# Attention loads in a fused attention, mixture and feed-forward kernel: v in four buffers a step sooner, converted blocks in two buffers

## The chip, the cores and the metric

The kernel runs on one core of a Trainium2 chip, as one launch. The metric is the device time of one execution in microseconds. The profile is of one execution, whose span runs from its first to its last instruction.

## What is computed

Three layers follow one another. The attention is a linear one with decay: for each of 4 batches and 8 heads, over 768 positions of width 64, in blocks of 64,

```python
intra = einsum('bhic,bhjc->bhij', qb, kb) * Dmask
out   = einsum('bhij,bhjd->bhid', intra, vb) + einsum('bhid,bhde->bhie', qb * lam_pow, kv_state)
kv_state = lam_block * kv_state + einsum('bhsd,bhse->bhde', kb * rev_pow, vb)
```

Its output, read as 3072 tokens of width 512, goes through a soft mixture of 8 experts (4 slots each, inner width 1024: logits against `phi`, a softmax over tokens that forms the slots, `relu(slot @ w1) @ w2` for each expert, a softmax over slots that spreads the results), and then through a feed-forward layer of width 2048 with the gate `h * sigmoid(1.702 h)`. The weights `w_in` and `w_out` of this last layer arrive as float64 bit patterns and are turned into float32 on the chip.

## The kernel before

**Attention.** A step takes one batch, one half of a sequence (`HS` = 384 rows, in three chunks of 128) and one pair of heads; there are `NSTEP` = 32 steps. Four steps with the same half form a group `g`; even groups are first halves, odd groups second halves. The order of all instructions is written out by hand in the loop at L534, which is a software pipeline: at step `i` it issues, among others, the scores of step i+1 (`do_SC`, TensorE L300, masked by VectorE at L303), the transposes of q and k of step i+2 (`do_T`, L262 and L264, copied out by ScalarE at L272 and L275), the transposes of step i-1's result (`do_XT`, L358), the product with the state (`do_XS`, L339), the state update of step i+1 (`do_ST`, TensorE L313 with v and the decayed k, then VectorE L322 and L324), the decayed k of step i+2 (`do_kd`, ScalarE L288) and the product with v of step i (`do_XA`, L347). In the first step of a group the logits and the slot sums of an earlier group come on top (`tail_logits` L368, `tail_z` L455, `tail_slot` L440, `tail_acc` L449); in the other steps there is less of such tail work. Each engine runs its instructions in the order in which they are issued.

**Loads.** Nearly all loads go through SP's queue, in order; a load into a buffer that is still in use waits there and holds those behind it. At step i SP issues q of step i+5 (L123), a piece of the expert weights (512 KB, L159 or L161, into one of 32 slots of 4 KB a partition), k of step i+5 (two loads, L128; three buffers, freed by `do_kd` of step i), in odd steps a float64 block (`load_early`, L228), and v of step i+3 (two loads, L128; three buffers, freed by `do_XA` of step i). v of step i+3 is first read by `do_ST` in step i+2.

**The float64 blocks.** Ten blocks (`EARLY`, 128 x 256 values; eight of `w_in`, two of `w_out`) are converted beside the attention. They all pass through one tile, `stage`, which is the first of the 32 weight slots and holds the block and a third part for the result's bits. Block c is loaded at step 2c+1 and converted at step 2c+2 (`do_early`): ScalarE takes the magnitude (L183), VectorE puts the bits together in three instructions (L192, L195, L198), GpSimd makes a mask of the magnitude (L205) and multiplies by it (L206). The weight piece 31, the last in the first round of slots, reuses the slot of `stage`.

**After attention.** At the last steps the pools of attention are freed and more slots are laid over them. The experts (L757, L775) read the pieces of weights; 64 pieces are loaded in all, the rest of them as buffers come free. Then follow the output stages (L1013 and L1179), bound to TensorE.

Of the kernel before, what the change touches and what calls it, by code (L numbers as in the profile page):

```python
# [8 lines left out]
F32 = mybir.dt.float32  # L9
F32R = mybir.dt.float32r  # L10
U32 = mybir.dt.uint32
# [6 lines left out]
def attention_moe_gelu_kernel(  # L18
# [14 lines left out]
    PE, ACT, DVE, POOL, SP = nc.tensor, nc.scalar, nc.vector, nc.gpsimd, nc.sync  # L33

    B, H, S, D = q.shape
    P = 128
# [13 lines left out]
    NSTEP = NG * NHP  # L50
    NE = 1
    NPC = 32
# [14 lines left out]
    CB = 256  # L67
# [5 lines left out]
    slots = slots_cm.__enter__()  # L73
# [3 lines left out]
    attn = attn_cm.__enter__()  # L77

    early_cm = tc.tile_pool(name="early", bufs=2, side="right", reuse_waits="tile")
    early = early_cm.__enter__()  # L80
# [27 lines left out]
    q_r, q_t, k_t, v_t = {}, {}, {}, {}  # L108

    def step_of(s):  # L110
        g, hp = divmod(s, NHP)
        b, hf = divmod(g, NHF)
        return b, hf, hp, g

    def load_step(s, what="qkv"):
        if s >= NSTEP:
            return
        b, hf, hp, g = step_of(s)
        t0 = hf * HS
        if "q" in what:  # L120

            q_r[s] = early.tile([P, 2, R * D], F32, tag="qr", name="qr", bufs=3)
            SP.dma_start(out=q_r[s], in_=q[b, 2 * hp:2 * hp + 2, t0:t0 + HS, :].rearrange("h (p c) d -> p h (c d)", p=P))  # L123
        for src, nm, ts, bufs, pool in ((k, "k", k_t, 3, early), (v, "v", v_t, 3, attn)):
            if nm in what:
                t = pool.tile([P, R, 2, D], F32, tag=nm, name=nm, bufs=bufs)
                for h in range(2):
                    SP.dma_start(out=t[:, :, h, :],  # L128
                                 in_=src[b, 2 * hp + h, t0:t0 + HS, :].rearrange("(c p) d -> p c d", p=P))
                ts[s] = t  # L130

    w_in32, w_out32 = w_in.bitcast(U32), w_out.bitcast(U32)
    staged = {}


    PC = 1024
# [42 lines left out]
    def convert_abs(key, mask=None):  # L179
        if mask is None:  # L180
            mask = ex.tile([P, DM], F32, tag="cvm", name="cvm", bufs=3)
        m = mask
        ACT.activation(out=m, in_=staged[key][:, :, 1].bitcast(F32), func=AF.Abs)  # L183
        magn[key] = m

    def conversion(key, out, guard):


        t, m = staged.pop(key), magn.pop(key)
        up, low = t[:, :, 1], t[:, :, 0]  # L190
        a = out.bitcast(U32) if key[0] != "early" else stage[:, 2 * CB:3 * CB]
        DVE.tensor_scalar(out=a, in0=up, scalar1=3, scalar2=0x3FFFFFFF,  # L192
                          op0=ALU.logical_shift_left, op1=ALU.bitwise_and)
        yield
        DVE.scalar_tensor_tensor(out=a, in0=up, scalar=0xC0000000, in1=a,  # L195
                                 op0=ALU.bitwise_and, op1=ALU.bitwise_or)
        yield
        DVE.scalar_tensor_tensor(out=a, in0=low, scalar=29, in1=a,  # L198
                                 op0=ALU.logical_shift_right, op1=ALU.bitwise_or)
        yield  # L200
        if guard is DVE:
            DVE.scalar_tensor_tensor(out=out, in0=m, scalar=F64_MIN, in1=a.bitcast(F32),
                                     op0=ALU.is_ge, op1=ALU.mult)
        else:
            POOL.tensor_scalar(out=m, in0=m, scalar1=F64_MIN, scalar2=None, op0=ALU.is_ge)  # L205
            POOL.tensor_tensor(out=out, in0=a.bitcast(F32), in1=m, op=ALU.mult)  # L206

    def by_turns(*work, rounds=9):

        work = list(work)  # L210
        while work and rounds:
            work = [w for w in work if next(w, 0) is None]
            rounds -= 1
        return work


    stage = slots.tile([P, PC], F32, tag="w", name="stage").bitcast(U32)

    NCW = 512 // CB

    EARLY = [(w_in32, kk * P, n * 512 + h * CB, w_in_sb[n][:, kk, h * CB:(h + 1) * CB])
             for n in range(NE) for kk in range(KD) for h in range(NCW)]
# [2 lines left out]

    def load_early(c):
        src, r, o, dst = EARLY[c]
        SP.dma_start(out=stage[:, :2 * CB], in_=src[r:r + P, 2 * o:2 * (o + CB)])  # L228
        staged["early", c] = stage[:, :2 * CB].rearrange("p (n t) -> p n t", t=2)

    def do_early(c):
        o = EARLY[c][-1]
        convert_abs(("early", c), o)
        by_turns(conversion(("early", c), o, POOL))
# [247 lines left out]
    with tc.manual_schedule():  # L482
# [7 lines left out]
        def warm_up(n):  # L490
            for _ in range(n):
                PE.matmul(bwarm, warm[:, :P], warm, start=True, stop=True)
# [5 lines left out]
        for h in range(2):  # L498
            r = slice(h * D, (h + 1) * D)
# [10 lines left out]
        n = 1  # L510
# [12 lines left out]
        def make_isum():  # L523
            for j in range(G):
                for i in range(G):
                    POOL.tensor_copy(out=isum4[i * NS:(i + 1) * NS, j, :],
                                     in_=ident[i * NS:(i + 1) * NS, i * NS:(i + 1) * NS])

        def load_pieces(i):
            n = min(NPC, max(0, i + 1) * NPC // (NSTEP - 1), NPC - 1 if i < NSTEP - 5 else NPC)  # L530
            while nxt_w[0] < n:
                load_piece()

        for i in range(-2, NSTEP):  # L534
            g, ph = divmod(i, NHP)
            if i > -2:
                load_step(i + 5, "q")
            if i == 1:
                make_isum()

            if 0 <= i + 1 < NSTEP:
                do_SC(i + 1)
            if 0 < i + 2 < NHP:

                for h in range(2):
                    make_dec(2 * (i + 2) + h)

            if 0 <= i + 2 < NSTEP:
                do_T(i + 2)
                if i == -2:  # L550
                    warm_up(1)
            if i == NSTEP - 1:
                do_XS(i)
            if 0 <= i - 1 < NSTEP:
                do_XT(i - 1)
            if 0 <= i + 3 < NSTEP:
                do_q(i + 3)
            if ph == 1 and 0 <= g - 1 < NG:
                tail_L(g - 1)
            if ph == 2 and 0 <= g - 1 < NG:  # L560
                tail_max(g - 1)
            if ph == 3 and 0 <= g - 1 < NG:
                tail_exp(g - 1)
            if i == NSTEP - 1:
                tail_logits_first(NG - 1)
            if 0 <= i < NSTEP - 1:
                do_XS(i)

            if 0 <= i + 1 < NSTEP:
                do_ST(i + 1)  # L570
            if 0 <= i + 2 < NSTEP:
                do_kd(i + 2)
            if 0 <= i < NSTEP:
                do_XA(i)

            if ph == 0 and 0 <= g - 1 < NG:
                tail_logits(g - 1)
            if ph == 0 and 0 <= g - 2 < NG:
                tail_z(g - 2, "tk")
                tail_slot(g - 2)  # L580
                tail_acc(g - 2)
            if i == NSTEP - 4:
                load_pieces(i + 1)

            load_pieces(i)

            load_step(i + 5, "k")
            c, turn = divmod(i - 2, EVERY)
            if turn == 1 and 0 <= c + 1 < len(EARLY):
                load_early(c + 1)  # L590
            if i >= 0:
                load_step(i + 3, "v")
            if 0 <= i + 2 < NSTEP:
                do_qd(i + 2)
            if i == -2:
                load_step(2, "v")
                SP.dma_start(out=phi_sb, in_=phi.rearrange("(k p) s -> p k s", p=P))
            if turn == 0 and 0 <= c < len(EARLY):
                do_early(c)
            if ph == 3 and 0 <= g - 1 < NG and i < NSTEP - 1:  # L600
                tail_row(g - 1)
            if ph == 0 and 0 <= g - 2 < NG:
                tail_row_exp(g - 2)
            if i == NSTEP - 2:
                early_cm.__exit__(None, None, None)
                slotb_cm = tc.tile_pool(name="slotb", bufs=NPC_B, side="right", reuse_waits="tile")
                slotb = slotb_cm.__enter__()

                rooms = [piece_room(NPC + j) for j in reversed(range(NPC_B))]
                while rooms:  # L610
                    load_piece(rooms.pop())
            if i == NSTEP - 1:
                attn_cm.__exit__(None, None, None)
                slotc_cm = tc.tile_pool(name="slotc", bufs=NPC_C, side="left", reuse_waits="tile")
                slotc = slotc_cm.__enter__()
                for _ in range(NPC_C):
                    load_piece()
# [288 lines left out]
        for kk in range(KD):  # L906
            src = bso[kk][:, None, :NS].to_broadcast([P, G, NS])
# [447 lines left out]
```

## Time and profile before

| | us |
|---|---|
| runs | 482.38, 485.71, 1572.84 (median 485.71) |
| the profiled execution | 483.99 |
| its span | 482.2 |
| TensorE busy in the span | 470.6 (98%) |
| VectorE busy | 375.5 (78%) |
| ScalarE busy | 302.8 (63%) |
| GpSimd busy | 76.4 (16%) |

The run of 1572.84 us is far from the others and is not used. The profiled execution lies between the two others. Busy shares are means over the whole span, in which attention, experts and output stages follow one another; matmuls are pipelined, so that a busy TensorE can still be waiting in between. The granted clock of TensorE is full over the span (mean 0.998). In the rows below, L12 is line 12 of the kernel; PEld is TensorE's weight load, SPq the sequencer of SP; a matmul group is named by the tile it writes (`bs` scores, `bst` state update, `bx` output, `bq` and `bk` transposes, `bp` slot sums).

### The profile page before, as it was taken

How to read it: one execution, taken by the hardware profiler on the slowest of the kernel's cores; microseconds unless marked ns; L12 is line 12 of the kernel's file. 1: busy time of each engine (PE TensorE's matmuls, PEld its weight loads, DVE VectorE, ACT ScalarE, POOL GpSimd, SP SyncE). 2: the span in 40 equal slices, each digit the busy share in tenths (PEclk: the TensorE clock that was granted, in tenths of full speed). 3: DMA queues.
4: the chain of work that ended last, by engine and by line, in shares of the span. 5: the costliest groups of instructions: out<-in, count | busy, mean ns of one | idle time of the engine just before them, and what ended most of it. 6: DMA issues, size and time to landing. Idle time of an engine off the chain costs nothing.

```text
span 482.2 us, 10665 instructions
## 1 busy us (share of the span) xinstructions
PE 470.6 (98%) x3991; PEld 391.7 (81%) x3991; DVE 375.5 (78%) x903; ACT 302.8 (63%) x605; POOL 76.4 (16%) x125
## 2 busy tenths in 40 slices
PE   8998999999999999999999999999999999999996
PEld 5877778778887443878788778888899999999996
DVE  4777778988875432897787598998779988888986
ACT  5786677777774126876865867676756565565551
POOL 3553344443230110000000000000001111011101
PEclk9999999999999999999999999999999999999999
DMA  8999989999899999246644542100222331233024
GB/s 185 250 286 275 270 256 293 282 260 295 235 306 354 410 407 369 89 159 238 220 130 130 189 133 98 63 0 2 88 88 36 54 44 15 32 45 45 4 43 88
DMA packets 81796, 81.52 MB, mean 169 GB/s; under 512 B 54736, under 2 KB 63440, under 8 KB 81744
## 3 DMA queue, kind: packets, MB, share of 16 engines
q1 hardware_dynamic: 79296, 76.63, 50.8%
q0 software_dynamic: 2304, 4.20, 6.4%
q8 instruction: 32, 0.52, 0.5%
q14 instruction: 20, 0.16, 0.1%
q10 hardware_dynamic: 144, 0.00, 0.0%
HBM read 69.80 MB, written 11.01 MB: 168 GB/s over the span
## 4 chain that ended last, share of the span: by engine, by line
PE 76%; DMA 12%; DVE 7%; SPq 2%; issue 1%; ACT 1%; DVEq 0%; ACTq 0%
PE bo L1013 26%; PE bp L1179 24%; DMA w<-in_moe_w_dram 9%; PE bs L300 4%; PE bx L347 3%; PE bx L339 2%; PE bsh L1135 2%; PE bhh L966 2%; PE bst L313 2%; DMA v<-in_v_dram 2%; PE bq L262 2%; PE bt L358 1%; SPq L128 1%; DMA stage<-in_moe_w_in_dram 1%; PE bk L264 1%
## 5 line engine op out<-in xcount | busy, mean ns | idle before, releaser
L1013 PE MATMUL bo<-wlo,GHI 128*128 128x512 f32 x192 | 75.3, 395 | 0.1
L1013 PE MATMUL bo<-whi,GLO 128*128 128x512 f32 x192 | 75.1, 394 | 0.0
L1013 PE MATMUL bo<-whi,GHI 128*128 128x512 f32 x192 | 74.8, 393 | 0.1
L1149 ACT ACTIVATE GHI<-G_all 128x896 fp32r<-128x896 f32 x48 | 45.8, 954 | 46.1 <-DVE G_all L1142 45.9
L1142 DVE TENSOR_TENSOR G_all<-G_all 128x128 f32<-128x128 f32 x192 | 47.4, 288 | 18.5 <-ACT G_all L1138 15.9
L1209 POOL DMA_DIRECT2D out_dram<-f x16 | 14.2, 1046 | 279.7 <-DVE G_all L1142 265.1
L1179 PE MATMUL bp<-tc,GHI 128*128 128x256 f32 x288 | 55.9, 282 | 0.0
L1154 DVE TENSOR_TENSOR GLO<-G_all,GHI 128x896 fp32r<-128x896 f32 x48 | 52.0, 1084 | 0.0
L974 ACT ACTIVATE G_all<-bhh 128x384 f32<-128x384 f32 x64 | 28.2, 489 | 34.6 <-PE bhh L966 34.5
L1179 PE MATMUL bp<-whi,GHI 128*128 128x256 f32 x192 | 49.5, 281 | 0.0
L1179 PE MATMUL bp<-wlo,GHI 128*128 128x256 f32 x192 | 49.2, 282 | 0.0
L1179 PE MATMUL bp<-whi,GLO 128*128 128x256 f32 x168 | 47.5, 283 | 0.0
L1179 PEld LDWEIGHTS bp<-tc,GHI 128*128 128x128 f32 x288 | 44.4, 190 | 0.0
L1013 PEld LDWEIGHTS bo<-wlo,GHI 128*128 128x128 f32 x192 | 36.0, 188 | 9.6 <-issue 2.5
L1013 PEld LDWEIGHTS bo<-whi,GLO 128*128 128x128 f32 x192 | 36.0, 188 | 7.8 <-DVE GLO L980 0.3
L1013 PEld LDWEIGHTS bo<-whi,GHI 128*128 128x128 f32 x192 | 36.1, 188 | 7.5 <-DVE W2s L920 0.5
L1179 PE MATMUL bp<-tc,GLO 128*128 128x256 f32 x144 | 40.4, 280 | 0.0
L980 DVE TENSOR_TENSOR GLO<-G_all,GHI 128x768 fp32r<-128x768 f32 x32 | 30.6, 955 | 10.5 <-ACT GHI L977 10.2
L281 POOL TENSOR_TENSOR qdT<-qT,qtab 128x384 f32<-128x384 f32 x32 | 32.1, 1002 | 38.7 <-PE bx L339 17.8
L300 PEld LDWEIGHTS bs<-qT,kT 64*128 64x128 f32 x384 | 26.7, 191 | 12.8 <-DVE zsum L460 4.2
L300 PE MATMUL bs<-qT,kT 64*128 64x128 f32 x384 | 33.3, 295 | 1.7 <-DVE AT L303 1.2
L303 DVE TENSOR_TENSOR AT<-bs,dec 128x384 f32<-128x384 f32 x64 | 32.5, 550 | 2.9 <-PE bs L300 2.2
(231 smaller groups left out, 1050.2 us busy)
## 6 DMA issues: line engine op xcount, KB each, us to landing
w<-in_moe_w_dram SPq DMA_DIRECT2D x64, 512.0 KB, 6.6
f<-in_moe_w_out_dram SPq DMA_DIRECT2D x15, 512.0 KB, 3.4
qr<-in_q_dram SPq DMA_DIRECT2D x32, 192.0 KB, 4.2
k<-in_k_dram SPq DMA_DIRECT2D x64, 96.0 KB, 4.4
v<-in_v_dram SPq DMA_DIRECT2D x64, 96.0 KB, 4.1
f<-in_moe_w_in_dram SPq DMA_DIRECT2D x12, 512.0 KB, 3.9
out_dram<-o SPq DMA_DIRECT2D x24, 256.0 KB, 2.4
out_dram<-f POOLq DMA_DIRECT2D x16, 256.0 KB, 4.6
```

The costliest lines, as they stand in the source:

```text
L281: POOL.tensor_tensor(out=qdT[s], in0=qT[s].rearrange("m (c i) -> m c i", c=R), in1=qtab[:, hp, None, :].to_broadcast([P, R, P]), op=ALU.mult)
L300: PE.matmul(bs[h][:, cs], kT[s][hs, cs], qT[s][hs, cs], start=True, stop=True)
L303: DVE.tensor_tensor(out=t, in0=bs[h][:, :HS].rearrange("m (c i) -> m c i", c=R), in1=dec[:, 2 * hp + h, None, :].to_broadcast([P, R, P]), ...
L347: PE.matmul(bx[h * D:(h + 1) * D, c * P:(c + 1) * P], v_t[s][:, c, h, :], AT[s, h][:, c, :], start=False, stop=(c == R - 1))
L974: ACT.activation(out=g[j][:, u * HS:(u + 1) * HS], in_=bh[j][u][:, :HS], func=AF.Gelu_apprx_sigmoid)
L980: DVE.tensor_tensor(out=glo[j][:, o], in0=g[j][:, o], in1=ghi[j][:, o].bitcast(F32), op=ALU.subtract)
L1013: PE.matmul(ob[t], a[j][:, t * P:(t + 1) * P], w[f], start=(begin and i == 0), stop=(end and i == 2))
L1142: DVE.tensor_tensor(out=o, in0=x, in1=y, op=op)
L1149: ACT.activation(out=sh[j], in_=gs(j)[:, P:], func=AF.Copy)
L1154: DVE.tensor_tensor(out=sl[j], in0=gs(j)[:, P:], in1=sh[j].bitcast(F32), op=ALU.subtract)
L1179: PE.matmul(bank_of(gi, i)[1], x, w, start=begin, stop=end)
L1209: POOL.dma_start(out=rows_of(gi, k), in_=cells[:, C11 + 2 * k:C11 + 2 * k + 2], accum_op=ALU.add)
```

## The change

v gets a fourth buffer, and its load at step i is that of step i+4 in place of i+3, from step -1 on in place of step 0, and stands ahead of the float64 block in SP's queue. The blocks alternate between two staging tiles, which take the first two of the 32 weight slots. A block is loaded at the same step as before and converted at step 2c+4 in place of 2c+2. The limit on the number of weight pieces before the last steps is 30 in place of 31.

```diff
@@ -121,7 +121,7 @@
 
             q_r[s] = early.tile([P, 2, R * D], F32, tag="qr", name="qr", bufs=3)
             SP.dma_start(out=q_r[s], in_=q[b, 2 * hp:2 * hp + 2, t0:t0 + HS, :].rearrange("h (p c) d -> p h (c d)", p=P))
-        for src, nm, ts, bufs, pool in ((k, "k", k_t, 3, early), (v, "v", v_t, 3, attn)):
+        for src, nm, ts, bufs, pool in ((k, "k", k_t, 3, early), (v, "v", v_t, 4, attn)):
             if nm in what:
                 t = pool.tile([P, R, 2, D], F32, tag=nm, name=nm, bufs=bufs)
                 for h in range(2):
@@ -188,7 +188,7 @@
 
         t, m = staged.pop(key), magn.pop(key)
         up, low = t[:, :, 1], t[:, :, 0]
-        a = out.bitcast(U32) if key[0] != "early" else stage[:, 2 * CB:3 * CB]
+        a = out.bitcast(U32) if key[0] != "early" else stage[key[1] % 2][:, 2 * CB:3 * CB]
         DVE.tensor_scalar(out=a, in0=up, scalar1=3, scalar2=0x3FFFFFFF,
                           op0=ALU.logical_shift_left, op1=ALU.bitwise_and)
         yield
@@ -214,7 +214,7 @@
         return work
 
 
-    stage = slots.tile([P, PC], F32, tag="w", name="stage").bitcast(U32)
+    stage = [slots.tile([P, PC], F32, tag="w", name="stage").bitcast(U32) for _ in range(2)]
 
     NCW = 512 // CB
 
@@ -225,8 +225,9 @@
 
     def load_early(c):
         src, r, o, dst = EARLY[c]
-        SP.dma_start(out=stage[:, :2 * CB], in_=src[r:r + P, 2 * o:2 * (o + CB)])
-        staged["early", c] = stage[:, :2 * CB].rearrange("p (n t) -> p n t", t=2)
+        t = stage[c % 2][:, :2 * CB]
+        SP.dma_start(out=t, in_=src[r:r + P, 2 * o:2 * (o + CB)])
+        staged["early", c] = t.rearrange("p (n t) -> p n t", t=2)
 
     def do_early(c):
         o = EARLY[c][-1]
@@ -527,7 +528,7 @@
                                      in_=ident[i * NS:(i + 1) * NS, i * NS:(i + 1) * NS])
 
         def load_pieces(i):
-            n = min(NPC, max(0, i + 1) * NPC // (NSTEP - 1), NPC - 1 if i < NSTEP - 5 else NPC)
+            n = min(NPC, max(0, i + 1) * NPC // (NSTEP - 1), NPC - 2 if i < NSTEP - 5 else NPC)
             while nxt_w[0] < n:
                 load_piece()
 
@@ -585,18 +586,18 @@
             load_pieces(i)
 
             load_step(i + 5, "k")
+            if i >= -1:
+                load_step(i + 4, "v")
             c, turn = divmod(i - 2, EVERY)
             if turn == 1 and 0 <= c + 1 < len(EARLY):
                 load_early(c + 1)
-            if i >= 0:
-                load_step(i + 3, "v")
             if 0 <= i + 2 < NSTEP:
                 do_qd(i + 2)
             if i == -2:
                 load_step(2, "v")
                 SP.dma_start(out=phi_sb, in_=phi.rearrange("(k p) s -> p k s", p=P))
-            if turn == 0 and 0 <= c < len(EARLY):
-                do_early(c)
+            if turn == 0 and 0 <= c - 1 < len(EARLY):
+                do_early(c - 1)
             if ph == 3 and 0 <= g - 1 < NG and i < NSTEP - 1:
                 tail_row(g - 1)
             if ph == 0 and 0 <= g - 2 < NG:
```

## Rows read from the trace of the kernel before

**Rows 1.** Page: chain that ended last, share by line.
```profile
PE bo L1013 26%; PE bp L1179 24%; DMA w<-in_moe_w_dram 9%; PE bs L300 4%; PE bx L347 3%; PE bx L339 2%; PE bsh L1135 2%; PE bhh L966 2%; PE bst L313 2%; DMA v<-in_v_dram 2%; PE bq L262 2%; PE bt L358 1%; SPq L128 1%; DMA stage<-in_moe_w_in_dram 1%; PE bk L264 1%
```

**Rows 2.** Same chain in order of time: start us, us, what.
```profile
159.80 10.14 DMA w<-in_moe_w_dram
```

**Rows 3.** Busy by stretch: us, PE PEld DVE ACT POOL, PEclk, DMA share, GB/s.
```profile
10.51:26.07 15.56, 14.87 (x189) 12.70 (x190) 12.84 (x39) 11.69 (x29) 8.67 (x22) 1.00 0.96 260
26.07:45.07 19.00, 17.65 (x206) 15.04 (x206) 12.75 (x37) 13.03 (x33) 8.11 (x10) 1.00 0.99 271
45.07:63.34 18.27, 17.43 (x219) 14.27 (x219) 15.00 (x48) 13.23 (x33) 7.32 (x10) 1.00 0.99 276
63.34:81.63 18.29, 18.13 (x219) 14.87 (x219) 14.66 (x43) 13.43 (x34) 8.05 (x11) 1.00 0.97 272
81.63:99.68 18.05, 17.50 (x220) 14.34 (x219) 16.41 (x51) 13.46 (x34) 7.78 (x11) 1.00 1.02 283
99.68:117.75 18.07, 18.07 (x220) 14.95 (x220) 14.83 (x44) 14.05 (x37) 7.33 (x10) 1.00 1.00 268
117.75:134.40 16.65, 16.65 (x220) 13.77 (x220) 14.37 (x44) 12.42 (x32) 4.58 (x6) 1.00 0.91 254
...
156.00:190.00 34.00, 32.92 (x400) 13.88 (x399) 12.92 (x44) 12.05 (x25) 3.38 (x11) 1.00 1.03 409
```

**Rows 4.** Waits, 8 to 112 us: engine line <- releaser: us, times, longest.
```profile
ACT w_in L183 <- DMA stage<-in_moe_w_in_dram: 11.3, 7, 2.3
DVE stage L192 <- DMA stage<-in_moe_w_in_dram: 8.0, 6, 2.4
PE bst L313 <- DMA v<-in_v_dram: 2.2, 5, 1.0
PEld bst L313 <- DMA v<-in_v_dram: 2.0, 3, 1.2
```

**Rows 5.** SP's queue, steps 13 to 14: start us, us, issue.
```profile
73.62 0.90 SPq L128 DMA_DIRECT2D k<-in_k_dram  x2
74.62 1.06 SPq L228 DMA_DIRECT2D stage<-in_moe_w_in_dram  x1
75.77 1.12 SPq L128 DMA_DIRECT2D v<-in_v_dram  x2
```

**Rows 6.** The chain there: start us, us, what.
```profile
69.30 0.87 PE bs L300 x12
73.34 0.87 PE bs L300 x12
75.77 4.40 DMA v<-in_v_dram
```

**Rows 7.** The chain in steps 24 and 25: start us, us, what.
```profile
122.16 0.89 PE bp L440 x6
123.05 0.87 PE bs L300 x12
126.98 0.87 PE bs L300 x12
```

**Rows 8.** Loads of v, 8 to 112 us, from issue to landing.
```profile
DMA to landing us min/median/max: 3.1/4.1/5.7
```

**Rows 9.** Work on the stage tile alone: us, DVE ACT POOL, clock, DMA.
```profile
8.00:112.00 104.00, 12.42 (x30) 4.38 (x10) 7.31 (x10) 1.00 0.98 270
```

**Rows 10.** Busy by stretch, 87.45 to 99.97 us (columns of rows 3).
```profile
87.45:99.97 12.52, 11.96 (x151) 10.56 (x151) 11.79 (x34) 8.71 (x21) 5.61 (x8) 1.00 1.02 283
```

**Rows 11.** VectorE in order of time: start us, us, instruction.
```profile
71.86 0.17 DVE L477 TENSOR_SCALAR rs<-rs 128x3 f32<-128x3 f32 x1
...
87.45 0.74 DVE L449 SCALAR_TENSOR_TENSOR acc<-acc,al,bp 96x512 f32<-96x512 f32 x1 [0.40 <-PE bp L440]
...
89.69 0.70 DVE L477 TENSOR_SCALAR rs<-rs 128x3 f32<-128x3 f32 x1
```

**Rows 12.** GpSimd in order of time: start us, us, instruction.
```profile
89.64 0.73 POOL L206 TENSOR_TENSOR w_in<-stage,w_in 128x256 f32<-128x256 f32 x1 [0.44 <-DVE stage L198]
```

## The prediction

> **What bounds the kernel now.** I read the chain that ended last first. By its shares [rows 1] most of the span is TensorE in the two output stages (L1013 and L1179, 50% together). The change does not touch these; they can only start sooner. Ahead of them the chain runs through loads of expert weights, one after another from 159.80 us on [rows 2], and the last stretch of rows 3 shows this stage at a DMA share of 1.03 and 409 GB/s. It is bound by its loads, which are asked for only as attention frees buffers, so it starts when attention ends. What attention saves therefore reaches the end of the span whole, and what is saved anywhere else is nothing.
>
> So the question is what the attention steps are bound by. The first seven windows cut attention into its groups of four steps [rows 3]: steps 0-3, 4-7, up to 24-27. The group at 117.75 has no conversion left: 16.65 us, TensorE busy for all of it. Groups alternate between first and second halves of a sequence; a step of the second half does one more state product and one state update less. Step 13 (second half) took 73.34 - 69.30 = 4.04 us [rows 6], step 25 with the same tail work (first half) 126.98 - 123.05 = 3.93 us [rows 7]. An undisturbed second-half group is thus about 16.65 + 4 x 0.11 = 17.1 us. Against these floors the groups stand at 19.00, 18.27, 18.29, 18.05 and 18.07 us [rows 3].
>
> The waits name two loads [rows 4]. TensorE waits for v at L313: 2.2 + 2.0 = 4.2 us over eight waits. ScalarE waits 11.3 us, and VectorE 8.0 us, for the float64 block that is to be converted; what stands behind the conversion in these engines (the copies of the transposes at L272, the masks at L303) is then late for TensorE. The queue says why [rows 5, 6]: the loads of step 13 were issued at 73.62 (k), 74.62 (float64 block) and 75.77 (v), since k and v wait for buffers that step 13 itself frees at its end. That v is for step 15's state update, and the chain has it landing 4.40 us later. Loads of v take 3.1 to 5.7 us [rows 8], so each lands about when it is wanted. The block is worse off: issued at the end of an odd step, wanted at the end of the next, some 4 us later.
>
> **The change, part by part.** *v in a fourth buffer, a step sooner.* The same 64 v loads with the same bytes. v(i+4) goes out in step i where v(i+3) did; with four buffers its wait is still for L347 of step i, so SP waits no longer than now. Its need lies one step (about 4 us) further off: some 9 us for a landing of at most 5.7 [rows 8]. The 4.2 us of rows 4 should go. One pair is issued in step -1 ahead of q(5) and a weight piece, about 1 us of SP's time at a point where k(5) waits for its buffer anyway: nothing. What is late next would be k(i+5), wanted two steps after its issue: not late.
>
> *The block fetched behind v.* SP passes the two v issues (1.12 us for the pair in rows 5) ahead of the block and 1.06 us or less of block after; q(i+6) behind both sees the same sum. The cost to the block is about 1 us of its new lead. *Converted three steps later, two buffers.* The block is loaded in the same step as now and wanted three steps later, about 12 us: the 11.3 and 8.0 us of waiting go. A load into a buffer now waits for a conversion that ended a step before, as now, so no new wait. The second buffer takes one weight slot; pieces 30 and 31 come to lie in the two stage slots at step 30, eight steps after the last conversion (step 22): nothing. The cap of 30 in place of 31 pieces never decides, as the other term gives at most 27 before step 27. The work itself stays: 12.42 / 10 = 1.24 us of VectorE for each conversion [rows 9], now in steps 4 to 22 in place of 2 to 20.
>
> That last point limits the gain. A first-half group needs 14.37 us of VectorE without conversions (seventh window) [rows 3], and with two 14.37 + 2.48 = 16.85, above TensorE's 16.65. The stretch from 87.45 to 99.97 has VectorE busy for 11.79 of 12.52 us [rows 10] and no wait for a load in it but 0.40 us for TensorE [rows 11]; there a faster load frees nothing. So group by group, by what is not VectorE's own work:
> - Steps 0-3, 15.56 us: TensorE's idle time is 15.56 - 14.87 = 0.69, and the conversion of step 2 leaves. I take 0.9 (0.69 to 1.2).
> - Steps 4-7, 19.00: no tail slots yet (0.89 us in rows 7), so the floor is 17.1 - 0.9 = 16.2; I take 16.3, a gain of 2.7 (from its idle time 1.35, to 2.8).
> - Steps 8-11, 18.27: first half, held by VectorE. 17.8, a gain of 0.5 (0 to 1.42, at 16.85).
> - Steps 12-15, 18.29: the v wait of step 15 goes, the lag from the group before stays. 17.6, a gain of 0.7 (0.16 of idle time, to 1.2).
> - Steps 16-19, 18.05: only what it inherits goes. 17.8, a gain of 0.25 (0 to 1.2).
> - Steps 20-23, 18.07, TensorE never idle: one conversion more than now, one late block less: 0 (0.3 lost to 1.0 gained).
>
> The sum is 0.9 + 2.7 + 0.5 + 0.7 + 0.25 = 5.05 us. The profiled execution took 483.99 us (span 482.2 and 1.8 around it): 483.99 - 5.05 = **478.9 us**. This execution lies between the two near runs, 482.38 and 485.71, the latter being the median shown. With the low ends it is 483.99 - 1.9 = 482.1, with the high ends 483.99 - 8.8 = 475.2.
>
> **Rivals.** *Transfers are the bound.* The six groups from 10.51 to 117.75 already have DMA shares of 0.96 to 1.02 [rows 3], weighted 106.06 of 107.24 us. If 1.02, the most that a whole group held, is the ceiling, attention can't fall below 106.06 / 1.02 = 104.0: a gain of 3.3 at most, and with a ceiling of 1.00 only 1.2. Between these, 2.3: 481.7 us. For it: the shares. Against it: the packets of large rows reach 1.03 in the last window [rows 3], and weight pieces, not wanted until the experts, can fall behind by a microsecond.
>
> *TensorE's floor is reached in all groups*, VectorE's lag having come from the late blocks alone: 475.2 us, the high ends above. Against it: rows 10.
>
> *The change does not do what it says*: the queue is so full that v, fetched sooner, lands later by as much. 484.0. Against it: the landings of rows 8 sit at 4.1 us in the median while the share is already near 1.
>
> *Slower.* GpSimd's part of a conversion blocks VectorE. Without the late load ScalarE's magnitude is early, GpSimd's mask is done ahead, and its product (0.73 us, L206) starts right behind VectorE's last step, under the small instructions that follow. That happened at 89.64 [rows 12]: L477, begun at 89.69, took 0.70 us and ended with the product, where it took 0.17 at 71.86 [rows 11]. If each of ten conversions held VectorE for a whole product, it would cost 7.3 us: 483.99 - 5.05 + 7.3 = 486.2. It decides from 0.51 us a conversion on. Against it: it can cost only where VectorE is the late engine, about half the conversions, and there rows 11 have it already. The Trainium skill, "SBUF — State Buffer", section "Who interferes with whom", says that GpSimd and VectorE share one port pair as an exclusive lock and that whichever starts first keeps it for its whole instruction; by that rule the small instruction has to wait whenever the product starts first, and the trace agrees (0.70 us against 0.17).
>
> **How the numbers follow.** My forecast 0.63, transfers 0.15, the floor 0.10, no effect 0.06, slower 0.06. The forecast's own range is 477.3 to 480.7, from half the distance to its bounds and less. The range to hold 8 of 10 goes from the floor to beyond the transfers: 475.2 to 483.0. A measurement tells 2%, some 9.7 us, from no change. No case but one beyond the floor gives that: faster 0.06, within 0.91, slower 0.03.
>
> **What would show it.** Right: no wait for v at L313 and none for the float64 block on ScalarE; steps 4-7 at about 16.3 us; steps 16-19 still near 17.8 with VectorE nearly full; the expert stage as long as before, about 5 us sooner. Wrong: a v or k wait left in the waits; DMA shares of 1.02 with TensorE idle in several groups; VectorE's small instructions at 0.7 us in most conversions; or a longer expert stage that gives back what attention saved.

## Result, and the profile after

| | before | after |
|---|---|---|
| median of 6 runs each | 484.57 us | 477.67 us |
| ratio | | 0.9882, interval 0.9859 to 0.9905 |
| the profiled execution | 483.99 us | 478.11 us |
| its span | 482.2 us | 476.1 us |

The ratio is of the fast runs alone, while the median before counts the far run of 1572.84 us too (484.02 us without it). The change saves 5.7 us by the ratio (1.2%, with its interval 4.6 to 6.8 us) and 5.9 us between the two profiled executions. The forecast of 478.9 us lies 1.2 us above the median. In the profile after, lines from L228 on stand one further down than before: the scores are L301, the state update is L314, the transposes of k are L265.

The groups of four steps after, in the columns of rows 3:

```profile
9.26:24.05 14.79, 14.04 (x189) 12.32 (x190) 12.15 (x39) 11.44 (x28) 8.16 (x21) 1.00 0.99 255
24.05:41.38 17.33, 16.60 (x209) 14.09 (x207) 12.46 (x36) 13.45 (x34) 7.33 (x9) 1.00 0.98 274
41.38:58.74 17.36, 17.08 (x220) 13.99 (x219) 15.26 (x47) 12.89 (x31) 6.75 (x10) 1.00 1.02 285
58.74:76.62 17.88, 17.88 (x218) 14.75 (x219) 15.38 (x45) 13.64 (x35) 8.49 (x12) 1.00 1.04 285
76.62:94.67 18.05, 17.09 (x220) 13.93 (x219) 16.36 (x51) 13.75 (x35) 8.00 (x11) 1.00 1.00 278
94.67:112.01 17.34, 17.34 (x221) 14.45 (x219) 14.70 (x43) 13.38 (x35) 7.99 (x11) 1.00 1.06 291
112.01:128.66 16.65, 16.65 (x220) 13.77 (x219) 14.69 (x46) 13.14 (x35) 5.08 (x7) 1.00 1.07 295
...
150.00:184.00 34.00, 33.02 (x401) 14.07 (x400) 13.04 (x44) 12.08 (x25) 3.39 (x11) 1.00 1.03 409
```

Read the first figure of each row against [rows 3]. The largest gain is in steps 4 to 7 (19.00 to 17.33), where it was forecast, though smaller. Steps 16 to 19 stay at 18.05, and steps 20 to 23, costed at nothing, gain 0.73 (0.66 if step 24 before is counted from its first matmul, at 117.68). The seventh group, which never had a conversion, is the same to 0.01 us. The expert stage still moves 409 GB/s.

The waits for loads that are left on TensorE and ScalarE, from 8 to 112 us (engine, line, releaser: us in total, times, longest):

```profile
ACT q L254 <- DMA qr<-in_q_dram: 4.8, 6, 1.2
PE bk L265 <- DMA k<-in_k_dram: 1.6, 2, 0.9
```

None is for v and none for a float64 block; those of [rows 4] are all gone from this execution. In their place stand q (4.8 us, on ScalarE) and k (1.6 us, on TensorE). The two waits for k are in steps 7 and 19. TensorE in order of time has them in brackets (start us, us, instruction, idle time before it and its releaser):

```profile
38.55 0.52 PE L265 MATMUL bk<-ident,k 128*128 128x128 f32 x3 [0.73 <-DMA k<-in_k_dram]
...
92.19 0.52 PE L265 MATMUL bk<-ident,k 128*128 128x128 f32 x3 [0.85 <-DMA k<-in_k_dram]
```

The k of the first of them, that of step 9, stands in SP's queue like this (start us, us, issue; two issues to a row):

```profile
32.22 2.08 SPq L128 DMA_DIRECT2D k<-in_k_dram  x2
34.40 0.96 SPq L128 DMA_DIRECT2D v<-in_v_dram  x2
```

The loop issues this k at step 4, whose decayed k had freed its buffer at 28.88:

```profile
28.09 0.79 ACT L289 ACTIVATE kd<-k,dec 128x192 f32<-128x192 f32 x2
```

It went out at 32.22, during the next step, and the pair of issues took 2.08 us instead of the 0.90 of [rows 5]. The chain has its second half, issued at 32.63, landing 5.79 us later, at 38.42, and TensorE starts on it at 38.55:

```profile
32.63 5.79 DMA k<-in_k_dram
```

The semaphores of the trace show one more thing that holds this queue. From 12 to 112 us, in every profile here, no load goes out before the eighth load before it in SP's queue has landed, so eight at most are on the way. The first half of this k went out at 32.22, once a weight piece had landed at 32.15, and the second at 32.63, once an earlier k had landed at 32.59. Such waits for weight pieces add up to 5.4 us after the change (8 to 112 us), to 1.4 before it:

```profile
SPq L128 <- DMA w<-in_moe_w_dram: 5.4, 16, 0.6
```

With v in four buffers the limit is the same as before. What sets it was not tried.

Behind attention nothing changed but the start. The first matmuls of the output stage (the tile `bhh`) run from 194.9 us before and 188.8 after, 6.1 us apart, like the spans (before, then after):

```profile
L966 PE MATMUL bhh<-cT,W2s x64: 334/338/440, 194.9 to 336.0; 128*128 128x384 f32 x64
```

```profile
L967 PE MATMUL bhh<-cT,W2s x64: 334/338/442, 188.8 to 329.9; 128*128 128x384 f32 x64
```

### The profile page after: what moved, and what is told of

It reads as the page before. It is cut to its first block, busy times and chain, and to the rows that moved or that the text cites. A ratio compares the mean times of both kernels' runs of the same rounds, so it can differ in the third digit from the quotient of the medians.

```text
span 476.1 us, 10660 instructions
## 1 busy us (share of the span) xinstructions
PE 465.3 (98%) x3991; PEld 388.0 (81%) x3991; DVE 375.5 (79%) x903; ACT 303.3 (64%) x605; POOL 76.5 (16%) x125
## 4 chain that ended last, share of the span: by engine, by line
PE 81%; DMA 10%; DVE 5%; SPq 1%; ACT 1%; issue 1%; DVEq 0%; ACTq 0%
PE bo L1014 26%; PE bp L1180 24%; DMA w<-in_moe_w_dram 7%; PE bs L301 4%; PE bx L348 3%; PE bx L340 3%; DMA k<-in_k_dram 2%; PE bsh L1136 2%; PE bq L263 2%; PE bst L314 2%; PE bhh L967 2%; PE bt L359 2%; PE bk L265 2%; PE bl L369 1%; PE bp L441 1%; SPq L128 1%
## 5 line engine op out<-in xcount | busy, mean ns | idle before, releaser
L273 ACT ACTIVATE qT<-bq 128x384 f32<-128x384 f32 x32 | 22.6, 707 | 20.1 <-PE bq L263 18.4
L1180 PEld LDWEIGHTS bp<-wlo,GHI 128*128 128x128 f32 x192 | 34.7, 189 | 0.0
L1180 PEld LDWEIGHTS bp<-whi,GHI 128*128 128x128 f32 x192 | 34.6, 189 | 0.0
```

The lines of the kernel that those rows point to most:

```text
L273: ACT.activation(out=t.rearrange("m (p c) -> m c p", c=R), in_=bq[:, :HS].rearrange("m (c p) -> m c p", c=R), func=AF.Copy)
L1180: PE.matmul(bank_of(gi, i)[1], x, w, start=begin, stop=end)
```

## Experiments

Each ratio is to runs of the kernel before that were made beside it; their medians lie between 482.65 and 483.0 us, 1 us and more below the 484.02 of the result. So kernels are compared by their ratios first: the change itself has 0.9882. "End of attention" is the start of the last step's scores in the profiled execution, before and after:

```profile
144.00 0.94 PE L300 MATMUL bs<-qT,kT 64*128 64x128 f32 x12
```

```profile
138.11 0.94 PE L301 MATMUL bs<-qT,kT 64*128 64x128 f32 x12
```

Each kernel has one profile, and single executions differ: the first run below ends attention 1.06 us sooner than the kernel before, at a ratio of 1.0018.

**One part alone: v.**

```diff
-        for ... (v, "v", v_t, 3, attn)):
+        for ... (v, "v", v_t, 4, attn)):
...
-            if i >= 0:
-                load_step(i + 3, "v")
+            if i >= -1:
+                load_step(i + 4, "v")
```

> The v part alone (four buffers, a step sooner, behind the block as before; blocks as before). Theory A, two separate waits: the 4.2 us of TensorE's waits for v go, the 13 us of ScalarE's and 8 us of VectorE's waits for blocks stay; it saves 1.5 to 2.5 of the 6 us. Rival B, transfers set the pace and any extra lead gives the whole: it saves 5 or more and the block waits shrink too. Rival C, the blocks' waits hide behind v: saves 4 to 6 with block waits unchanged.

Measured: 483.12 us, ratio 1.0018 (0.9991 to 1.0044). Fetching v sooner is worth nothing that can be measured alone, which none of the three cases had. No wait for v is left, but those for the float64 block stay: the longest on ScalarE grows from 2.3 us [rows 4] to 3.5, and it falls early. ScalarE and then TensorE in order of time:

```profile
24.77 0.43 ACT L183 ACTIVATE w_in<-stage 128x256 f32<-128x256 f32 x1 [3.54 <-DMA stage<-in_moe_w_in_dram]
...
26.79 2.02 PE L300 MATMUL bs<-qT,kT 64*128 64x128 f32 x12 [2.96 <-DVE AT L303]
```

The conversion waits 3.54 us for its block, the masks behind it on VectorE are late, and TensorE stands for 2.96 us. Then the twelve scores take 2.02 us, where 0.94 is usual (the rows at 144.00 and 138.11). The stretch shows why:

```profile
26.00:33.00 7.00, 6.21 (x43) 5.79 (x45) 3.26 (x10) 4.06 (x11) 2.57 (x4) 0.52 1.04 284
```

The granted clock is 0.52 in it, near TensorE's lower level (1.2 GHz is 0.50), after TensorE had been idle. Steps 3 and 4 took 6.52 and 7.40 us, where the kernel after takes 3.48 and 4.49. This suggested that v was worth something and the clock ate it. The next run takes the clock's fall away.

**v alone, with TensorE kept busy in that wait.** As above, and:

```diff
+            if i == 3:
+                bfill = bank("m", "bfill")
+                for _ in range(12):
+                    PE.matmul(bfill, warm[:, :P], warm, start=True, stop=True)
```

> The v part alone once more, with 12 matmuls on constants (bf16, into a bank that is free there) behind step 3's products, where TensorE stood idle for 3 us for the first block and its granted clock then read 0.50 for some 6 us. Theory A, the clock ate what the v part saved: the clock stays at 1.00, step 4 takes 4.5 to 5.5 us in place of 7.4, and 1.5 to 2.5 us are saved against the v part alone (480.5 to 481.5). Rival, the late block alone ate it: step 4 gets no shorter and the time stays within 0.7 of the v part alone.

Measured: 484.68 us, ratio 1.0035 (1.0011 to 1.0059). The clock stayed at 1.00 through the stretch, and the first two groups took 33.40 us instead of 36.86 (2.0 us sooner at their end, as they began 1.5 us later). Yet it did not help. The waits for the block then come later, on ScalarE 13.1 us in eight waits, where v alone without the filler had 9.2 in six:

```profile
ACT w_in L183 <- DMA stage<-in_moe_w_in_dram: 13.1, 8, 3.0
```

The three groups from step 8 on took 17.96, 18.51 and 18.99 us, 2.5 more than with v alone (17.21, 17.82, 17.92). With v alone they had been as short as after the change; in that execution its loss lay in steps 3 and 4. So the idea that the clock ate v's gain is not borne out. Nor do the single runs of v alone bear it out: the two with a mean clock of 0.998 and more took 482.98 and 482.44 us, like the kernel before. As long as the block is wanted a step after it is issued, it is waited for, in one place or another.

**The other part alone: the blocks.** The change, with v as before.

```diff
-        for ... (v, "v", v_t, 4, attn)):
+        for ... (v, "v", v_t, 3, attn)):
...
-            if i >= -1:
-                load_step(i + 4, "v")
+            if i >= 0:
+                load_step(i + 3, "v")
```

> The block part alone (two staging tiles, converted three steps later; v as before in three buffers, behind the block). Theory A: the block waits go, TensorE's waits for v stay at 3 to 5 us; it saves 3.5 to 4.5 us. Rival B (any lead gives the whole): 5 or more and few v waits. Rival C (v is the wait that counts): under 2.

Measured: 481.22 us, ratio 0.9970 (0.9944 to 0.9996), some 1.4 us saved. That is the time of rival C, but its reason, v as the wait that counts, does not fit the run of v alone. The block's waits are gone, v's stay:

```profile
PE bst L314 <- DMA v<-in_v_dram: 1.7, 3, 0.8
PEld bst L314 <- DMA v<-in_v_dram: 1.7, 4, 0.9
```

Alone the parts give 0 and 1.4 us, together 5.7. They are two waits on the same steps, before the change in steps 3, 7 and 15, and with the blocks alone the waits for v stand in these three again. Step 7, before (ScalarE, TensorE) and then here:

```profile
42.28 0.44 ACT L183 ACTIVATE w_in<-stage 128x256 f32<-128x256 f32 x1 [2.33 <-DMA stage<-in_moe_w_in_dram]
...
43.92 0.50 PE L313 MATMUL bst<-v,kd 128*64 128x64 f32 x9 [1.03 <-DMA v<-in_v_dram]
```

```profile
41.77 0.82 PE L314 MATMUL bst<-v,kd 128*64 128x64 f32 x11 [0.70 <-DMA v<-in_v_dram]
```

Where one is taken away, the other ends last.

**The order in the queue.** The block ahead of v, as before the change:

```diff
-            if i >= -1:
-                load_step(i + 4, "v")
             c, turn = divmod(i - 2, EVERY)
             if turn == 1 and 0 <= c + 1 < len(EARLY):
                 load_early(c + 1)
+            if i >= -1:
+                load_step(i + 4, "v")
```

> The changed kernel with the block's load ahead of v again in SP's queue. Theory A: both have more than a step of lead, so the order is worth nothing: within 1 us of the changed kernel (477 to 479). Rival: the order carries part of the gain: 2 us or more slower, with waits for v back.

Measured: 477.29 us, ratio 0.9898 (0.9866 to 0.9929). The order is worth nothing that can be measured, as the prediction had it. In this profile TensorE waits for no k, though all ten blocks are loaded, and steps 4 to 7 take 16.40 us; one wait for v (0.5 us) is back:

```profile
24.08:40.48 16.40, 16.40 (x208) 14.12 (x207) 12.43 (x36) 13.41 (x34) 7.53 (x9) 1.00 1.08 298
```

The time does not change either when the weight piece, not wanted until the experts, goes last:

```diff
-            load_pieces(i)
-
...
                 load_early(c + 1)
+            load_pieces(i)
```

> The changed kernel with the weight piece issued last in a step, behind k, v and the block. The changed kernel still waits for k in steps 7 and 19 (1.0 us each) and ScalarE for q (4.8 us). Theory A, SP's queue as a whole runs about a step behind because transfers fill it: the cyclic order is nearly the same, the waits for k and q stay in sum, within 1 us of the changed kernel. Rival: the 512 KB piece just ahead of k is what makes it late: the waits for k go and 1.5 to 2 us are saved more (about 476).

Measured: 477.43 us, ratio 0.9899 (0.9865 to 0.9934). k now goes out ahead of the piece, and its waits are gone, as the rival had it, but without a gain; q, behind the piece, is waited for instead:

```profile
ACT q L254 <- DMA qr<-in_q_dram: 13.1, 16, 1.4
```

**How much VectorE's work is worth.** Two of VectorE's three instructions of each conversion are left out:

```diff
+        if key[0] != "early":
             DVE.scalar_tensor_tensor(out=a, in0=up, scalar=0xC0000000, in1=a, ...
             ...
             DVE.scalar_tensor_tensor(out=a, in0=low, scalar=29, in1=a, ...
```

> The changed kernel without the second and third of VectorE's three instructions in each of the ten early conversions (left out: putting the sign and the low bits in; about 0.92 us of VectorE each). Theory A, VectorE holds the first-half groups: steps 8-11 and 16-19 fall by 0.6 us each or more, second-half groups by 0.2 to 0.4; in all 1.5 to 2.5 us under the changed kernel. Rival, transfers hold all groups: under 0.7 us.

Measured: 475.54 us, ratio 0.9845 (0.9823 to 0.9867): some 2 us below the change. The two first-half groups that VectorE held (steps 8 to 11 and 16 to 19) fall to the floor of the seventh group:

```profile
40.63:57.28 16.65, 16.65 (x220) 13.77 (x218) 14.65 (x46) 12.88 (x33) 7.51 (x11) 1.00 1.08 299
...
74.60:91.26 16.66, 16.66 (x221) 13.77 (x219) 14.74 (x46) 12.95 (x33) 7.51 (x11) 1.00 1.05 294
```

TensorE is busy for all of both, at DMA shares of 1.08 and 1.05. So those groups were held by VectorE, not by transfers. (In this execution steps 20 to 23 took 18.62 us, with a wait for k in step 23.)

**GpSimd beside VectorE.** The conversion without GpSimd's mask and product:

```diff
+        last = out.bitcast(U32) if key[0] == "early" else a
-        DVE.scalar_tensor_tensor(out=a, in0=low, scalar=29, in1=a,
+        DVE.scalar_tensor_tensor(out=last, in0=low, scalar=29, in1=a,
...
+        if key[0] == "early":
+            return
```

> The changed kernel without GpSimd's two instructions (mask and product) in the early conversions; VectorE's third instruction writes the result (left out: small values are no longer set to zero). Theory A, the blocking of VectorE's small instructions is real but short: the 0.70 us instruction of the row sums is 0.17 in all steps, and 0.5 to 1.2 us are saved in all. Rival, it costs more than that all over: 2 us or more. Rival, it costs nothing on the path: within 0.3.

Measured: 477.59 us, ratio 0.9881 (0.9857 to 0.9905), the same as with GpSimd's part. The small instruction `rs` of the slot tail, six times in each kernel (ns shortest/median/longest, first and last start), first before, then after, then here:

```profile
L477 DVE TENSOR_SCALAR rs<-rs x6: 169/170/707, 54.1 to 141.0; 128x3 f32<-128x3 f32 x6
```

```profile
L478 DVE TENSOR_SCALAR rs<-rs x6: 169/702/706, 48.9 to 135.1; 128x3 f32<-128x3 f32 x6
```

```profile
L481 DVE TENSOR_SCALAR rs<-rs x6: 168/169/170, 48.8 to 134.2; 128x3 f32<-128x3 f32 x6
```

The median rose from 170 to 702 ns with the change and is 169 without GpSimd's part. The hold-up came about as the slower rival said, and it cost nothing that the times can show. On the path it does show, in the two first-half steps right behind this instruction: steps 10 and 18 take 4.09 and 4.07 us after the change and 3.72 and 3.71 here. After the change the instruction stands ahead of the masks for step 10, on a VectorE that is late:

```profile
48.94 0.71 DVE L478 TENSOR_SCALAR rs<-rs 128x3 f32<-128x3 f32 x1
```

So some 0.7 us in all come from this, less than the interval of the ratios (1.1 us to either side).

**Fewer bytes.** Eight of the ten blocks are not loaded; their conversions stay and read what the tiles hold.

```diff
+        if c < 2:
             SP.dma_start(out=t, in_=src[r:r + P, 2 * o:2 * (o + CB)])
```

> The changed kernel with only the first two of the ten float64 blocks loaded; all ten conversions run, on the blocks that lie there (left out: 8 loads of 256 KB). Theory A, transfers fill the queue and so make k late in steps 7 and 19 and q late for ScalarE: these waits go, 1 to 2.5 us are saved. Rival, VectorE and TensorE hold all that is left: within 0.5.

Measured: 477.25 us, ratio 0.9883 (0.9863 to 0.9904). No wait for k is left; steps 7 and 19 take 4.05 and 4.04 us in place of 4.97 and 4.75. Then step 20 takes 5.89 instead of 5.41: VectorE, which had caught up during the wait for k, is late again. Attention ends at 136.96, 1.15 us sooner in the profiled execution, and the ratio does not tell the two kernels apart. That the blocks' bytes made k late is not shown by this: with the block ahead of v, and without GpSimd's part, all ten blocks were loaded and no k was late either.

**More lead for k and q.** From step 1 to 20, k and q are fetched a step sooner, every fourth pair into a spare slot of the weights:

```diff
-                load_step(i + 5, "q")
+                for s in ahead_of_step(i):
+                    load_step(s, "q")
...
-            load_step(i + 5, "k")
+            for s in ahead_of_step(i):
+                load_step(s, "k")
```

> The changed kernel with k and q a step sooner too for steps 6 to 26 (a fourth buffer of each in a third reserved weight slot). Theory A, only the lead was short: the waits for k (2 us of steps 7 and 19) and q (4.8 us of ScalarE) go, 1 to 2 us are saved (475.5 to 476.5). Rival, the transfers themselves are full: the waits move to another load or stay, within 0.7 us of the changed kernel.

Measured: 480.02 us, ratio 0.9942 (0.9921 to 0.9963), some 2.4 us slower than the change. The waits for v are back:

```profile
PEld bst L321 <- DMA v<-in_v_dram: 1.5, 2, 1.1
PE bst L321 <- DMA v<-in_v_dram: 1.1, 2, 0.9
```

The extra q and the extra pair of k at step 1 stand ahead of v in the same queue. The lead given to k and q is taken from v, which has less to spare: step 4 takes 5.68 us in place of 4.49. That is not all of the loss: attention ends only 0.74 us later than after the change (138.85), the output stage starts 2.0 us later:

```profile
L983 PE MATMUL bhh<-cT,W2s x64: 334/338/443, 190.8 to 331.9; 128*128 128x384 f32 x64
```

So over 1 us is lost behind attention, where the spare slot leaves the weights one slot less until the last steps. This was not tried apart.

**The conversions where VectorE has room.** Blocks are loaded and converted at chosen steps, the even (first-half) groups left with few or none:

```diff
+        LOAD_AT = (1, 3, 5, 6, 8, 13, 14, 16, 21, 22)
+        CONV_AT = (4, 5, 7, 12, 13, 15, 20, 21, 23, 27)
...
-            if turn == 1 and 0 <= c + 1 < len(EARLY):
-                load_early(c + 1)
+            if i in LOAD_AT:
+                load_early(LOAD_AT.index(i))
...
-            if turn == 0 and 0 <= c - 1 < len(EARLY):
-                do_early(c - 1)
+            if i in CONV_AT:
+                do_early(CONV_AT.index(i))
```

> The changed kernel with the ten conversions moved into second-half groups (steps 4, 5, 7, 12, 13, 15, 20, 21, 23 and 27), loads at steps 1, 3, 5, 6, 8, 13, 14, 16, 21 and 22. Theory A, VectorE holds the first-half groups only: steps 8-11 and 16-19 fall to 16.6 to 16.9 us, the other groups stay within 0.3, and 1.3 to 2 us are saved against the changed kernel (about 476). Rival, the transfers take it back as late k or v: within 0.7 of the changed kernel. Rival, the second-half groups become bound by VectorE: slower than the changed kernel.

Measured: 478.23 us, ratio 0.9912 (0.9878 to 0.9945). The first-half groups fall to 16.88 and 16.65 us, but some blocks have only two steps of lead, and their waits come back, with steps 12 to 15 at 18.44:

```profile
ACT w_in L183 <- DMA stage<-in_moe_w_in_dram: 1.5, 2, 1.3
```

Two kernels mend this. One spreads the ten further, with one conversion in the last step of each first-half group from step 8 on (11, 19 and 27):

```diff
-        LOAD_AT = (1, 3, 5, 6, 8, 13, 14, 16, 21, 22)
-        CONV_AT = (4, 5, 7, 12, 13, 15, 20, 21, 23, 27)
+        LOAD_AT = (1, 3, 5, 7, 12, 14, 16, 20, 22, 24)
+        CONV_AT = (4, 6, 11, 13, 15, 19, 21, 23, 27, 28)
```

> The changed kernel with conversions at steps 4, 6, 11, 13, 15, 19, 21, 23, 27 and 28, each fetched three steps or more before: at most one in a first-half group, in its last step. Theory A, VectorE's place in the group is what is left to gain, and the late blocks took it back in the run before: steps 8-11 and 16-19 at 16.6 to 16.9 us, steps 12-15 and 20-23 at 17.3 to 17.9, no wait for a block; 1 to 2 us saved against the changed kernel (475.7 to 476.7). Rival, transfers give it back later: within 0.7 of the changed kernel.

Measured: 477.83 us, ratio 0.9902 (0.9873 to 0.9931). The groups of steps 8 to 23:

```profile
40.90:57.55 16.65, 16.65 (x220) 13.77 (x218) 14.37 (x44) 12.40 (x32) 4.59 (x7) 1.00 1.05 289
57.55:74.88 17.33, 17.33 (x221) 14.45 (x219) 14.67 (x44) 13.79 (x36) 7.90 (x11) 1.00 1.11 302
74.88:91.53 16.65, 16.65 (x221) 13.77 (x219) 15.39 (x47) 12.73 (x33) 6.09 (x9) 1.00 1.04 282
91.53:108.85 17.32, 17.32 (x221) 14.44 (x219) 14.64 (x44) 13.78 (x36) 7.88 (x11) 1.00 1.00 267
```

TensorE is never idle in any of them, and no wait for a load is left from 8 to 112 us. The other uses three staging tiles:

```diff
-    stage = [... for _ in range(2)]
+    stage = [... for _ in range(3)]
...
+        LOAD_AT = (1, 3, 4, 8, 10, 12, 15, 17, 18, 20)
+        CONV_AT = (4, 6, 7, 12, 14, 15, 19, 21, 22, 23)
```

> The changed kernel with three staging tiles and conversions at steps 4, 6, 7, 12, 14, 15, 19, 21, 22 and 23, fetched three steps or more before: as the run before, with none after step 23. Theory A, the late conversions cost the last steps and the weight pieces behind them: attention ends as early or earlier, the expert stage is as long as in the changed kernel, and 1.5 to 2.5 us are saved (475.2 to 476.2). Rival, the transfers are full up to the experts' end and give it back there: within 0.8 of the changed kernel, with attention ending 2 us or more sooner all the same.

Measured: 478.19 us, ratio 0.9898 (0.9862 to 0.9934). In both, attention ends some 2.3 us sooner than after the change (135.64 and 135.90 against 138.11), and the median does not show it. The output stage of the first and of the second, against 188.8 with the change:

```profile
L970 PE MATMUL bhh<-cT,W2s x64: 334/338/443, 187.5 to 328.6; 128*128 128x384 f32 x64
```

```profile
L970 PE MATMUL bhh<-cT,W2s x64: 334/338/447, 187.3 to 328.6; 128*128 128x384 f32 x64
```

It starts only 1.3 and 1.5 us sooner: from the end of attention to it pass 51.9 and 51.4 us, where it is 50.7 after the change and 50.9 before. About 1 us is given back there, which the loads of the experts bound. The rest, 1.3 us or so, is seen in the profiled executions (477.19 and 477.22 us against 478.11), and intervals of 1.4 to 1.7 us to either side can't show it. By its time this is the rival of the last kernel; its reason, transfers that are full up to the experts' end, is not shown. With the short conversions attention ended as early (135.98), and from there to the output stage passed only 50.3 us:

```profile
L968 PE MATMUL bhh<-cT,W2s x64: 334/338/440, 186.3 to 327.4; 128*128 128x384 f32 x64
```

So the 1 us may lie in what these two moved: conversions as late as step 28 in the one, a third tile in place of a weight slot in the other. Which it is was not tried. No version here beats the change by more than its uncertainty, but for the one that leaves work out.

## Why the prediction was right, point by point

- *What bounds the kernel.* "What attention saves therefore reaches the end of the span whole" held for this change: 5.89 us at the end of attention, 6.1 at the output stage, 6.1 in the span. It held with the short conversions too, and not with the last two kernels, which give back about 1 us.
- *The sum.* It came out close in part by luck. The six groups gave 4.49 us for the 5.05 forecast, and 1.25 us came from an earlier start, which no term has. The sum also starts from one execution of 483.99 us, where later medians of the kernel before are 482.65 to 483.0.
- *v and block waits go.* Both went, as forecast. That each alone would leave the other in place is not in the prediction; the runs of the single parts show it. The gains by group are thus not shares of two edits that could be priced apart.
- *Steps 0 to 3*, 0.9 forecast: 0.77 in the window. Step 0 also began 1.25 us sooner, which belongs to neither part: kernels with the same first steps begin it at 9.0 to 9.5 or at 10.3 to 10.7 us, and most of those that begin sooner spend 0.5 to 1.2 us more in step 0 itself (4.10 us here, 3.28 before). Start and first group together, 2.0 us of the 5.9 come from before step 4. In the three later kernels that fetch as the change does up to step 3 and begin late, the group takes 14.20 us, 1.36 less than before: by them the term was too small, and the rest of the 2.0 us is the start.
- *Steps 4 to 7*, 2.7 forecast: 1.67. This is the term that was mis-sized, by 1 us, and the step of it that failed is "What is late next would be k(i+5), wanted two steps after its issue: not late." The prediction counted the lead from the step that the loop issues k in. SP ran a step behind the loop, and the pair's issue took 2.08 us, so that k had about 5.6 us to its need (37.82) instead of 8, and landed 6.2 us after its issue began. It is not so in every execution. With two blocks, but also with the block ahead of v and without GpSimd's part, step 7 takes 4.05 us and the group 16.40, where 16.3 was forecast. So the floor was right; what makes k late in one profile and not in the other stays open.
- *Steps 8 to 15*, 0.5 and 0.7 forecast: 0.91 and 0.41, together 1.3 for 1.2.
- *Steps 16 to 19*, 0.25 forecast: 0. The wait for k in step 19 (0.85 us) took what was inherited. *Steps 20 to 23*, 0 forecast: 0.73, since VectorE caught up in that wait. The run with two blocks has both the other way round: 17.34 and 17.88 us. The two errors cancel but for 0.5 us.
- *VectorE limits the first halves.* Shown: with two thirds of VectorE's conversion instructions left out, or with the conversions moved, these groups fall to 16.65 us with TensorE never idle. Its own 17.8 for steps 8 to 11 was a little high (17.36). The sum behind it, 14.37 + 2.48 = 16.85 us of VectorE, does not hold group by group: VectorE is busy for 15.26 us in steps 8 to 11 and 16.36 in steps 16 to 19. It is late in single steps, around a conversion, and not over the whole group.
- *Transfers are the bound.* Its ceiling of 1.02 falls: the groups after hold 1.04, 1.06 and 1.07, and the spread conversions 1.11 at 302 GB/s. What is left of this rival is shorter: a full queue makes single loads late.
- *Slower, by GpSimd.* The Trainium skill, "SBUF — State Buffer", section "Who interferes with whom", was borne out in size and place: 702 ns in place of 170 for the small instruction. The prediction's reason against the rival held too: it costs something only where VectorE is late (0.37 us in each of steps 10 and 18), part of which the kernel before paid already (0.70 us at 89.69 [rows 11]), and without GpSimd's part the time is the same within the interval. It had the price at 0.51 us a conversion to decide; the path shows 0.7 us in all.
- *The range.* Its ends, 475.2 and 483.0, came from the floor in all groups and from the transfers. The floor is real, though 17.3 us in second halves and not 17.1: the spread conversions reach it from step 4 to step 23 with TensorE never idle in steps 8 to 23, and their profiled execution still took 477.19 us, as not all arrives.

## What to carry to other kernels

Where two loads are late in the same steps, neither need be worth its wait alone: taking one away shows the other, and here only the pair paid (0 and 1.4 us, 5.7 together). A load's lead is counted from where its queue really is, by the issue times in the trace, and not from the step in which the program issues it; a full queue can be a whole step behind. The queue can also have a limit of its own: here eight loads on the way at most, before and after v had its fourth buffer. And in one shared queue lead given to one load can be taken from another: a step more for k and q brought v's waits back, in a kernel that was 2.4 us slower.

## What had not been expected of the hardware

- The DMA share of a stretch is not capped near 1.02 as [rows 3] had suggested: it held 1.11 at 302 GB/s over 17 us with TensorE never idle.
- The issue of a pair of loads on SP takes 0.90 us at its shortest and, in the profile after, up to 2.25 us (at 24.25 us, at a DMA share of 0.98 over the group); each such issue holds up the loads behind it in the queue.
- An idle stretch of 3 us on TensorE early in attention was followed by 6.2 us at a granted clock of 0.53 (26.79 to 33.00 us), in which the twelve scores took 2.02 us instead of 0.94. With TensorE kept busy instead, the step behind the stretch took 4.49 us in place of 7.40: in that execution the clock's fall cost 2.9 us, as much as the wait itself.
